# An SSM convolution by FFT with its gradients and a bilinear GLU: FFT stages in another order, buffers used in place, PSUM copies shared by ScalarE and VectorE

## Chip, cores and metric

The kernel runs on one core of one Trainium2 chip. The metric is device time in microseconds (us) of one execution of the whole program; the time of a version is the median over its runs. Engines are named as the profile names them: PE (TensorE; PEld is its weight load), DVE (VectorE), ACT (ScalarE), POOL (GpSimd), SP (SyncE, whose queue issues every DMA here).

## What is computed

One layer's forward pass and all its gradients, in bfloat16, for 2048 positions and 512 channels (F = 1376). x is normalized, passes through a long convolution (by FFT of length 4096) with a short shift filter and gates around it, and, beside that, through a bilinear GLU:

```python
def A(q, k, v, shift_k, ssm_k, ssm_D):
    k_shift = sum(k_pad[:, t:t + S, :] * shift_k[:, ks - 1 - t] for t in range(4))
    kv = k_shift * v
    y = irfft(rfft(kv, 2 * S) * rfft(ssm_k, 2 * S))[:S]
    return q * (y + kv * ssm_D)

def B(x, w_gate, w_up, w_down):
    return ((x @ w_gate) * (x @ w_up)) @ w_down

xn = layernorm(x)
out = x + A(xn, k, v, shift_k, ssm_k, ssm_D) + B(xn, w_gate, w_up, w_down)
# outputs: out, and by vjp with grad_out the gradients of
# x, k, v, shift_k, ssm_k, ssm_D, w_gate, w_up, w_down
```

Output numbers in the code: out_0 is the layer's output; out_1 to out_3 the gradients of x, k, v; out_4 of the shift filter; out_5 of ssm_k; out_6 of ssm_D (512 numbers of two bytes); out_7 to out_9 of the three weights.

## The kernel before

**Tools.** Tile pools assign buffers and every semaphore; each engine then runs its instructions in one fixed order, waiting where an instruction's input or buffer is not ready. Large tiles come from three rings of SBUF buffers, and a new tile waits until an old one of its ring has been read for the last time, by DMAs too: `s32` (four buffers), `c16` (two) and `z24` (one). PSUM tiles of the first half come from one ring of four (`ps2`).

```python
340         return main.tile(shape, dt, name=name, tag="s32", bufs=4)
343         return main.tile(shape, dt, name=name, tag="c16", bufs=2)
346         return main.tile(shape, dt, name=name, tag="z24", bufs=1)
```

**Part one, FFTs (L372 to L459).** Each transform is three steps on PE, each followed by copies out of PSUM that alternate between ACT and DVE (`evac`): `c_to_T` transposes [channel, time] data (64 transposes, 4 copies), `fwd_f1` is the first FFT factor (128 matmuls, 16 copies), `fwd_f2` the second (128 matmuls, 16 copies). Three signals are transformed: h (ssm_k, result H), kv (result KV) and dy = grad_out * xn (result DY). Order: h through all three steps; x_nat's statistics on DVE (L411) and normalization on ACT (L421, sixteen instructions), stored to xn_d for later; the shift filter as 64 matmuls with diagonal weights on k_pad (L433) into ks_C; `c_to_T` of ks_C into T_kv; v_T is loaded, multiplied into T_kv (L443); f1 and f2 of kv; xn_T and go_T are loaded and multiplied (L455); f1 and f2 of dy. The tables F2M (for f2) are made meanwhile by ACT (sines) and DVE (masks L110, copies L135, L137).

**Part two, inverses (L461 to L510).** Three times: DVE multiplies two spectra in sixteen pieces (`pointwise`), PE does `inv_i1` (copies into Bp by ACT), then `inv_i2` with table G2M, copied by ACT into y_C, dkv_C or dh_C, tiles of the c16 ring. y goes to yT_d in DRAM, dkv to dkvC_d, dh to out_5, and its first column to out_6. G2M has the z24 buffer, after F2M. Weights are loaded and transposed on PE in between: WdT (copies L504) and WT (copies L525, L528), all copied by ACT. y_nat, the transposed y, is loaded by one transposing DMA (L530) after that.

**Part three, the loop (L734 to L839).** Eight passes of 256 rows. natbuf holds rows of x, xn, grad_out (L555); PE transposes them, DVE copies them into zbuf (L565), PE multiplies by the gate and up weights (L749), ACT copies (L752), DVE forms the gated product (L758), and so on to out_0 and out_1. zbuf takes the z24 buffer. It also holds the slots A, B and C into which `apost_load` brings dkv, ks and (by a transposing DMA, L706) v; DVE works on these (L604, L613, L617, L619) to make the gradients of v, k and the shift filter. **Part four** (L843 to L895) makes the weight gradients on PE.

## Time and profile before

| | us |
|---|---|
| median of 6 runs | 756.66 (754.06 to 760.17) |
| the profiled execution | 757.93 |
| its span | 756.0 |
| PE busy | 603.1 (80%) |
| DVE busy | 427.3 (57%) |
| ACT busy | 358.3 (47%) |
| POOL busy | 16.8 (2%) |

The mean granted clock of PE over the span is 0.919 of full speed. Times in the views count from the start of the span. A busy share is a mean over parts with different limits, so the rows further down are read part by part: where the engine that ends a part sat idle, and what ended that idle time.

### The profile page before, as it was taken

The page shows a single profiled execution, that of the slowest core. Times are in us where ns is not written, and L with a number is a line of the kernel's source. Part 1 is how long each engine was busy: PE and PEld are TensorE (multiplying, and loading weights), DVE is VectorE, ACT ScalarE, POOL GpSimd, SP SyncE. Part 2 cuts the span into 40 slices and gives each one's busy share as a digit, 9 for nine tenths or more (in the row PEclk, how much of TensorE's full clock was granted, in tenths as well). Part 3 has the DMA queues.
Part 4 walks back from the last instruction along what each step waited for, and adds up shares of the span by engine and source line. Part 5 has one row for each costly group of instructions (what it writes and reads, how often), then busy time and mean ns, then how long its engine had stood idle before and what let it go on. Part 6 is the DMA issues. An engine that isn't in the chain of part 4 may idle for free.

```text
span 756.0 us, 13973 instructions
## 1 busy us (share of the span) xinstructions
PE 603.1 (80%) x5956; PEld 426.0 (56%) x5956; DVE 427.3 (57%) x952; ACT 358.3 (47%) x474; POOL 16.8 (2%) x21
## 2 busy tenths in 40 slices
...
GB/s 268 67 2 41 264 98 152 3 1 2 3 114 127 140 186 68 211 38 115 140 179 100 111 138 184 82 115 133 184 82 121 105 191 292 344 341 166 75 1 75
DMA packets 129469, 95.60 MB, mean 126 GB/s; under 512 B 78784, under 2 KB 118400, under 8 KB 129152
## 3 DMA queue, kind: packets, MB, share of 16 engines
...
## 4 chain that ended last, share of the span: by engine, by line
PE 43%; DVE 23%; DMA 12%; ACT 11%; SPq 8%; issue 2%; DVEq 0%; ACTq 0%
PE ps_wg L889 10%; PE ps_g L749 5%; PE ps_wd L878 5%; SPq L706 4%; PE ps_x L809 4%; PE ps_x L807 4%; ACT zbuf L630 3%; PE ps_o L793 3%; PE ps_n L692 3%; PE ps L207 2%; DVE pw_m L244 2%; DMA zbuf<-in_A_k_dram 2%; DVE pw_m L241 2%; DVE pw_m L242 2%; DMA zbuf<-dkvC_d 2%
## 5 line engine op out<-in xcount | busy, mean ns | idle before, releaser
L749 PE MATMUL ps_g<-zbuf,WgWu 128*128 128x256 bf16 (+1 forms) x704 | 82.0, 276 | 7.7 <-ACT btmp L752 6.7
L749 PEld LDWEIGHTS <-WgWu 128*128 128x128 bf16 (+1 forms) x704 | 70.2, 101 | 17.9 <-issue 9.2
L809 PE MATMUL ps_x<-WT,btmp 128*128 128x512 bf16 (+1 forms) x176 | 68.8, 391 | 0.0
L807 PE MATMUL ps_x<-WT,btmp 128*128 128x512 bf16 (+1 forms) x176 | 68.8, 391 | 0.0
L183 ACT CAST Bp<-ps 128x1024 bf16<-128x1024 f32 x48 | 49.9, 1103 | 35.6 <-PE ps L265 35.3
L752 ACT CAST btmp<-ps_g 128x512 bf16<-128x512 f32 x80 | 45.0, 584 | 41.3 <-PE ps_g L749 40.8
L889 PEld LDWEIGHTS <-xn_nat 128*128 128x128 bf16 x384 | 37.5, 98 | 36.9
L697 ACT COPY sf_stg<-ps_n 128x1376 bf16<-128x1376 bf16 x24 | 31.3, 1306 | 56.0 <-PE ps_n L692 50.9
L692 PE MATMUL ps_n<-ident,btmp 128*128 128x128 bf16 (+1 forms) x528 | 41.3, 222 | 16.1 <-DVE sf_stg L695 13.1
L692 PEld LDWEIGHTS <-btmp 128*128 128x128 bf16 (+1 forms) x528 | 34.0, 99 | 31.5 <-issue 13.9
L793 PE MATMUL ps_o<-WdP,btmp 128*128 128x512 bf16 (+1 forms) x176 | 44.5, 387 | 0.0
L766 PE MATMUL ps_dh<-zbuf,WdP 128*128 128x256 bf16 (+1 forms) x352 | 42.4, 272 | 0.0
L891 ACT CAST wstage<-ps_wg 128x512 bf16<-128x512 f32 (+1 forms) x24 | 13.0, 541 | 61.2 <-PE ps_wg L889 61.2
L814 ACT ACTIVATE dxn<-ps_x 128x512 f32<-128x512 f32 x16 | 9.6, 597 | 57.3 <-PE ps_x L811 37.5
L766 PEld LDWEIGHTS <-WdP 128*128 128x128 bf16 (+1 forms) x352 | 33.9, 100 | 3.4
L619 DVE SCALAR_TENSOR_TENSOR zbuf<-zbuf,wc 128x512 bf16<-128x512 bf16 x48 | 34.8, 744 | 0.4
L629 DVE TENSOR_TENSOR zbuf<-zbuf 128x512 bf16<-128x512 bf16 x64 | 23.6, 420 | 18.3 <-ACT zbuf L630 14.0
L262 PE MATMUL ps<-I1M,Y1c 128*64 128x128 bf16 x128 | 21.8, 250 | 14.9 <-DVE Y1c L245 14.9
L564 PE MATMUL ps_t<-ident,natbuf 128*128 128x128 bf16 x128 | 12.9, 230 | 23.7 <-DMA natbuf<-xn_d 21.5
L630 ACT ACTIVATE zbuf<-zbuf 128x2048 bf16<-128x2048 bf16 x16 | 30.8, 1925 | 1.6 <-DVE zbuf L629 1.6
L207 PE MATMUL ps<-BD,T_kv 128*64 128x256 bf16 x128 | 11.0, 342 | 23.5 <-DVE T_kv L443 23.5
L809 PEld LDWEIGHTS <-btmp 128*128 128x128 bf16 (+1 forms) x176 | 17.7, 100 | 19.8 <-issue 1.8
(194 smaller groups left out, 1522.6 us busy)
## 6 DMA issues: line engine op xcount, KB each, us to landing
...
h_sf<-h_n SPq DMA_DIRECT2D x2, 2048.0 KB, 9.9
dg_sf<-dg_n SPq DMA_DIRECT2D x2, 2048.0 KB, 17.1
du_sf<-du_n SPq DMA_DIRECT2D x2, 2048.0 KB, 16.6
...
```

The lines of the kernel that those rows point to most:

```text
L183: nc.scalar.copy(out=out, in_=in_)
L619: nc.vector.scalar_tensor_tensor(out=A_[:, s0:s0 + APC], in0=C_[:, s0 + j:s0 + j + APC], scalar=wc[:, t, j:j + 1], in1=A_[:, s0:s0 + APC], ...
L630: nc.scalar.activation(out=A_[:, 0:S], in_=A_[:, 0:S], func=ACTF.Copy, accum_out=dw[:, t, j:j + 1])
L692: nc.tensor.transpose(out=ps[:, ft * P:ft * P + fs], in_=XT[0:fs, ft, sl * P:(sl + 1) * P], identity=ident[0:fs, 0:fs])
L749: nc.tensor.matmul(ps[0:fs, ft - fa, :], lhsT=W[:, dt, ft * P:ft * P + fs], rhs=xg[:, 0, dt, :], start=(dt == 0), stop=(dt == NT - 1))
L752: nc.scalar.copy(out=dst[:, fa:fb, :], in_=ps[:])
L766: nc.tensor.matmul(ps[0:fs, ft - fa, :], lhsT=WdT[:, dt, ft * P:ft * P + fs], rhs=xg[:, 1, dt, :], start=(dt == 0), stop=(dt == NT - 1))
L793: nc.tensor.matmul(ps[:], lhsT=hT[0:fs, ft, sl * P:(sl + 1) * P], rhs=Wd[0:fs, ft, :], start=(ft == 0), stop=(ft == NFT - 1))
L807: nc.tensor.matmul(ps2[:], lhsT=dgT[0:fs, ft, sl * P:(sl + 1) * P], rhs=WgT[0:fs, ft, :], start=(ft == 0), stop=False)
L809: nc.tensor.matmul(ps2[:], lhsT=duT[0:fs, ft, sl * P:(sl + 1) * P], rhs=WuT[0:fs, ft, :], start=False, stop=False)
L878: nc.tensor.matmul(ps[0:fs, :], lhsT=sf_view(h_sf, h_rem, ft * P, fs)[:, st, :], rhs=go_nat[:, st, :], start=(st == 0), stop=(st == NST - 1))
L889: nc.tensor.matmul(ps[:, 0:fw], lhsT=xn_nat[:, st, dt * P:(dt + 1) * P], rhs=sf_view(main_t, rem_t, f0, fw)[:, st, :], start=(st == 0), st ...
```

## The change

Parts three and four keep their code; the rest changes so:

- The shift filter's matmuls come before f2 of h, and read and write one tile k_C (s32) in place; the upper half of each channel block is done first, and columns before time zero are skipped by shorter matmuls instead of a zeroed pad.
- v_T moves from the c16 ring to the s32 ring and is loaded right after k.
- f2 of h comes after `c_to_T` of k_C and the T_kv product's code.
- The z24 tile of part two, zinv, holds G2M and beside it io_t, into which all three inverses are copied and from which their stores read.
- y_nat is allocated and loaded right after y is stored.
- Two of the four WdT copies and half of the large WT copies go to DVE.
- A flag pool_assist lets POOL do one of the pointwise products; no line sets it.

```diff
+        self.pool_assist = False
...
-            nc.vector.tensor_tensor(out=m[3][:], in0=v(X, 1), in1=v(H, 0), op=ALU.mult)
+            (nc.gpsimd if self.pool_assist else nc.vector).tensor_tensor(out=m[3][:], in0=v(X, 1), in1=v(H, 0), op=ALU.mult)
...
-    k_pad = s32([P, NT, SP_], BF, "k_pad")
+    k_C = s32([P, NT, S], BF, "k_C")
...
+    v_T = s32([P, 64, P], BF, "v_T")
+    for t, src in enumerate(t_view(vv)):
+        nc.sync.dma_start(out=v_T[32 * t:32 * t + 32, :, :], in_=src)
...
     f.fwd_f1(T_h, A, "np")
-    H = s32([P, 128, 2, 32, 2], BF, "H")
-    f.fwd_f2(A, H)
...
-        for sc2 in range(S // 1024):
+        for sc2 in reversed(range(S // 1024)):
...
-                    nc.tensor.matmul(ps[:, u, :], lhsT=wdiag[:, t, j, :], rhs=k_pad[:, t, PAD - j + s0: PAD - j + s0 + 512],
+                    lo = j if s0 == 0 else 0
+                    nc.tensor.matmul(ps[:, u, lo:512], lhsT=wdiag[:, t, j, :], rhs=k_C[:, t, s0 + lo - j:s0 + 512 - j],
...
-            f.evac(out=ks_C[:, t, sc2 * 1024:(sc2 + 1) * 1024], in_=ps[:].rearrange("p u s -> p (u s)"))
+            f.evac(out=k_C[:, t, sc2 * 1024:(sc2 + 1) * 1024], in_=ps[:].rearrange("p u s -> p (u s)"))
...
-    v_T = c16([P, 64, P], BF, "v_T")
...
     nc.vector.tensor_tensor(out=T_kv[:], in0=T_kv[:], in1=v_T[:], op=ALU.mult)
+    H = s32([P, 128, 2, 32, 2], BF, "H")
+    f.fwd_f2(A, H)
...
-    C["G2M"] = z24([P, 64, 2, 32], BF, "G2M")
+    zinv = z24([P, 64 * 2 * 32 + NT * S], BF, "zinv")
+    C["G2M"] = zinv[:, 0:64 * 2 * 32].rearrange("p (a b c) -> p a b c", a=64, b=2)
+    io_t = zinv[:, 64 * 2 * 32:].rearrange("p (t s) -> p t s", t=NT)
...
+    f.inv_i2(Bp, io_t)
+    nc.sync.dma_start(out=yT_d.rearrange("(t p) s -> p t s", p=P), in_=io_t)
+    y_nat = c16([P, NST, D], BF, "y_nat")
+    nc.sync.dma_start_transpose(out=y_nat[:], in_=yT_d[:, :])
...
-        nc.scalar.copy(out=WdT[:, dt, :], in_=ps[:, 0:FF])
+        (nc.scalar.copy if dt % 2 == 0 else nc.vector.tensor_copy)(out=WdT[:, dt, :], in_=ps[:, 0:FF])
...
-                nc.scalar.copy(out=WT[:, w, f4:f4 + nfull, :], in_=ps[:, 0:nfull, :, :].rearrange("p a b c -> p a (b c)"))
+                (nc.scalar.copy if (f4 // 4 + w) % 2 == 0 else nc.vector.tensor_copy)(
+                    out=WT[:, w, f4:f4 + nfull, :], in_=ps[:, 0:nfull, :, :].rearrange("p a b c -> p a (b c)"))
```

The diff does not show where the scheduler puts each instruction. Three places of DVE's order do. The first is the start, around the two T_h copies (PSUM to SBUF after `c_to_T` of h); ln_stats and ln_mv belong to x_nat's statistics, cb_mi are index masks. Before:

```order
L110 TENSOR_SCALAR cb_mi_158<-cb_mi_158 128x32
L185 COPY T_h<-ps_258 128x2048
L411 BN_STATS ln_stats<-x_nat 128x6 x2
L110 TENSOR_SCALAR cb_mi_171<-cb_mi_171 128x1024
L185 COPY T_h<-ps_294 128x2048
```

Now:

```order
L412 BN_STATS ln_stats<-x_nat 128x6
L110 TENSOR_SCALAR cb_mi_176<-cb_mi_176 128x1024
L413 BN_AGGR ln_mv<-ln_stats 128x2 x2
L412 BN_STATS ln_stats<-x_nat 128x6 x2
L135 COPY F2M<-cb_resb_179 64x16x64 x2
L413 BN_AGGR ln_mv<-ln_stats 128x2 x2
L412 BN_STATS ln_stats<-x_nat 128x6
L110 TENSOR_SCALAR cb_mi_187<-cb_mi_187 128x1024
L186 COPY T_h<-ps_263 128x2048
L186 COPY T_h<-ps_299 128x2048
```

One T_h copy stood ahead of all statistics and the other behind one pair of them; now seven BN_STATS (three of them ahead of the rows shown) and two masks precede both.

The second place is the middle: from the last copies of T_kv to the first transform of kv. Before:

```order
L185 COPY T_kv<-ps_830 128x2048
L81 TENSOR_SCALAR cb_mi_1547<-cb_mi_1547 128x1024
L443 TENSOR_TENSOR T_kv<-T_kv,v_T 128x8192
L185 CAST A_kv<-ps_865 128x64x16
L185 CAST A_kv<-ps_885 128x64x16
```

Now:

```order
L186 COPY T_kv<-ps_672 128x2048
L186 CAST H<-ps_702 128x2x128x4
L186 CAST H<-ps_722 128x2x128x4
L81 TENSOR_SCALAR cb_mi_1545<-cb_mi_1545 128x1024
L186 CAST H<-ps_742 128x2x128x4
L440 TENSOR_TENSOR T_kv<-T_kv,v_T 128x8192
L186 CAST H<-ps_762 128x2x128x4
L186 CAST H<-ps_782 128x2x128x4
```

DVE's eight copies of H now lie around the T_kv product, three ahead of it and five behind; on PE, f2 of H lies between `c_to_T` of k_C and f1 of kv.

The third place is the start of the loop; the names behind "waits" are semaphores (DMAHW0 to 7 count DMAs, others an engine's instructions). Before:

```order
L611 MEMSET zbuf 128x8 [waits PE_49]
L604 TENSOR_TENSOR zbuf<-zbuf 128x512 [waits DMAHW7_49,DMAHW0_49]
L604 TENSOR_TENSOR zbuf<-zbuf 128x512 x3
L613 TENSOR_TENSOR zbuf<-zbuf 128x512 [waits DMAHW1_49]
L613 TENSOR_TENSOR zbuf<-zbuf 128x512 x3
L617 TENSOR_SCALAR zbuf<-zbuf,wc 128x512 [waits DVE_49] x2
L796 TENSOR_TENSOR a_t<-natbuf,y_nat 128x512 [waits DMAHW4_49,DMAHW3_49]
L619 SCALAR_TENSOR_TENSOR zbuf<-zbuf,wc 128x512 [waits DVE_49]
L803 TENSOR_TENSOR dxa<-natbuf,y_nat 128x512 [waits DMAHW4_49]
L565 COPY zbuf<-ps_t 128x8x128 [waits PE_49,Activation_49]
```

Now:

```order
L526 COPY WT<-ps_4273 128x1024 [waits PE_49]
L565 COPY zbuf<-ps_t 128x8x128 [waits DMAHW3_49,DMAHW4_49,DMAHW0_49,DMAHW6_49,PE_49,Activation_49]
L611 MEMSET zbuf 128x8
L565 COPY zbuf<-ps_t 128x8x128 [waits DVE_49,PE_49]
L604 TENSOR_TENSOR zbuf<-zbuf 128x512 [waits DMAHW6_49,DMAHW5_49]
L604 TENSOR_TENSOR zbuf<-zbuf 128x512 x3
L613 TENSOR_TENSOR zbuf<-zbuf 128x512 [waits DMAHW7_49]
L613 TENSOR_TENSOR zbuf<-zbuf 128x512 x3
L617 TENSOR_SCALAR zbuf<-zbuf,wc 128x512 [waits DVE_49] x2
L619 SCALAR_TENSOR_TENSOR zbuf<-zbuf,wc 128x512 [waits DVE_49] x6
L617 TENSOR_SCALAR zbuf<-zbuf,wc 128x512 x2
L758 TENSOR_TENSOR btmp<-btmp 128x2560 [waits Activation_49]
```

The two L565 copies moved ahead of the work on the slots; the first of them is now the first write into zbuf and waits for DMAs (DMAHW3 and DMAHW4 count those of out_6 and out_5), and L758 follows six of the twelve L619. On SP's queue the six natbuf loads moved from behind L706 to right behind y_nat's load.

## Rows read from the trace of the kernel before

**Rows 1.** The chain that ended last, in order of time: start us, us, engine, output.

```profile
72.41 7.53 DMA xn_d<-x_nat
...
88.80 10.67 DMA v_T<-in_A_v_dram
...
123.84 9.77 DMA go_T<-in_grad_out_dram
...
290.39 19.89 SPq L706
...
319.63 11.12 PE ps_g L749 x84
```

**Rows 2.** Timeline of PE, 54 to 116: start, us, instruction, [idle before <-releaser].

```profile
54.70 14.00 PE L433 MATMUL ps<-k_pad,wdiag 128*128 128x512 bf16 x64
...
74.24 6.45 PE L194 MATMUL ps<-ident,ks_C 128*128 128x128 bf16 x64 [5.53 <-ACT ks_C L183]
...
104.16 10.99 PE L207 MATMUL ps<-BD,T_kv 128*64 128x256 bf16 x128 [23.47 <-DVE T_kv L443]
```

**Rows 3.** Timeline of ACT: x_nat normalized, and the WdT copies.

```profile
61.00 11.38 ACT L421 ACTIVATE x_nat<-x_nat,ln_nmr,rstd 128x512 bf16<-128x512 bf16 x16
...
276.07 4.93 ACT L504 COPY WdP<-ps 128x1376 bf16<-128x1376 bf16 x4 [5.12 <-PE ps L503]
```

**Rows 4.** Timeline of SP's queue: start, us of issue, line, transfer, count.

```profile
106.84 13.62 SPq L451 DMA_DIRECT2D xn_T<-xn_d  x4
...
285.61 0.40 SPq L510 DMA_DIRECT2D out_dram<-dh_C  x1
...
288.36 0.39 SPq L508 DMA_DIRECT2D out_dram<-dh_C  x1
```

**Rows 5.** DMA issues: transfer, queue, kind, count, KB, median us to landing.

```profile
ksC_d<-ks_C SPq DMA_DIRECT2D x1, 2048.0 KB, 12.0
...
yT_d<-y_C SPq DMA_DIRECT2D x1, 2048.0 KB, 8.5
...
out_dram<-dh_C SPq DMA_DIRECT2D x1, 2048.0 KB, 18.1
...
zbuf<-in_A_v_dram SPq DMA_TRANSPOSE x4, 6.7
...
y_nat<-yT_d SPq DMA_TRANSPOSE x1, 14.1
...
out_dram<-dh_C SPq DMA_DIRECT2D x1, 1.0 KB, 16.0
```

**Rows 6.** Timeline of DVE: statistics, mask, F2M copies, go_T product, zbuf copy, gating product.

```profile
17.63 1.28 DVE L411 BATCH_NORM_STATS2 ln_stats<-x_nat 128x6 f32<-128x512 bf16 x2
...
19.52 0.69 DVE L110 TENSOR_SCALAR cb_mi<-cb_mi 128x1024 int32<-128x1024 int32 x1 [0.61 <-ACT cb_mi L109]
...
22.59 0.85 DVE L135 COPY F2M<-cb_resb 64x1024 bf16<-64x1024 bf16 x2
...
133.93 4.43 DVE L455 TENSOR_TENSOR go_T<-go_T,xn_T 128x8192 bf16<-128x8192 bf16 x1 [2.05 <-DMA go_T<-in_grad_out_dram]
...
316.97 0.69 DVE L565 COPY zbuf<-ps_t 128x1024 bf16<-128x1024 bf16 x1 [0.32 <-PE ps_t L564]
...
331.40 1.49 DVE L758 TENSOR_TENSOR btmp<-btmp 128x2560 bf16<-128x2560 bf16 x1 [5.07 <-ACT btmp L752]
```

**Rows 7.** Busy time by stretch: stretch, us, engines busy, PEclk, DMA share, GB/s.

```profile
21.40:35.00 13.60, 11.31 (x128) 9.83 (x128) 13.40 (x21) 13.02 (x13) 1.05 (x1) 1.00 0.30 55
116.40:131.90 15.50, 14.15 (x128) 12.44 (x128) 9.80 (x9) 8.10 (x8) 0.00 (x0) 1.00 1.38 155
215.00:238.00 23.00, 18.52 (x411) 15.37 (x405) 23.00 (x69) 14.92 (x16) 0.00 (x0) 0.85 0.24 93
300.00:306.50 6.50, 0.00 (x0) 0.00 (x0) 0.00 (x0) 0.00 (x0) 0.00 (x0) 0.50 0.93 322
```

**Rows 8.** Costliest groups of instructions, from the page: the L619 chain.

```profile
L619 DVE SCALAR_TENSOR_TENSOR zbuf<-zbuf,wc 128x512 bf16<-128x512 bf16 x48 | 34.8, 744 | 0.4
```

More of the change, by code (lines that the diff above doesn't have):

```diff
@@ L439 @@
     f.c_to_T(ks_v, T_kv)
-    v_T = c16([P, 64, P], BF, "v_T")
-    for t, src in enumerate(t_view(vv)):
-        nc.sync.dma_start(out=v_T[32 * t:32 * t + 32, :, :], in_=src)
     nc.vector.tensor_tensor(out=T_kv[:], in0=T_kv[:], in1=v_T[:], op=ALU.mult)
-    A = s32([P, 2, 32, 256], BF, "A_kv")
-    f.fwd_f1(T_kv, A, "np")
+    H = s32([P, 128, 2, 32, 2], BF, "H")
+    f.fwd_f2(A, H)
+    A2 = s32([P, 2, 32, 256], BF, "A_kv")
+    f.fwd_f1(T_kv, A2, "np")
     KV = s32([P, 128, 2, 32, 2], BF, "KV")
-    f.fwd_f2(A, KV)
+    f.fwd_f2(A2, KV)
     xn_T = s32([P, 64, P], BF, "xn_T")
@@ L473 @@
         f.inv_i1(Y1, Bp, jq0=j0 // 8, jq1=(j0 + JC) // 8, jbase=j0)
-    y_C = c16([P, NT, S], BF, "y_C")
-    f.inv_i2(Bp, y_C[:])
-    nc.sync.dma_start(out=yT_d.rearrange("(t p) s -> p t s", p=P), in_=y_C[:])
+    f.inv_i2(Bp, io_t)
+    nc.sync.dma_start(out=yT_d.rearrange("(t p) s -> p t s", p=P), in_=io_t)
+    y_nat = c16([P, NST, D], BF, "y_nat")
+    nc.sync.dma_start_transpose(out=y_nat[:], in_=yT_d[:, :])
     Bp = s32([P, 64, 2, 128], BF, "Bp2")
@@ L480 @@
         f.inv_i1(H, Bp, jq0=j0 // 8, jq1=(j0 + JC) // 8)
-    dkv_C = c16([P, NT, S], BF, "dkv_C")
-    f.inv_i2(Bp, dkv_C[:])
-    nc.sync.dma_start(out=dkvC_d, in_=dkv_C[:])
+    f.inv_i2(Bp, io_t)
+    nc.sync.dma_start(out=dkvC_d, in_=io_t)
     WgWu = s32([P, 2, NT, FF], BF, "WgWu")
```

14 lines of the change are left out of this document (4 added, 10 removed).

## The prediction

> **What bounds the kernel now.** I read the chain of waits in order of time first, because it names the stretches where nothing computes; then each engine's timeline around those stretches; then the DMA issues, for what the waits wait on. The tail (weight gradients) and most of the eight-pass loop are PE work that the diff does not touch. The diff touches what comes before the loop's first matmul at 319.63 [rows 1]. There the chain shows three holes.
>
> Hole one: the transposes of the shifted k (L194) begin at 74.24, having sat idle 5.53 us for the last ks_C copies [rows 2]. These stood on ACT behind the sixteen x_nat normalizations, 11.38 us from 61.00 [rows 3]. Hole two: the next matmuls start at 104.16 after 23.47 us of idle [rows 2]. Their input waits for v_T, whose DMA takes over x_nat's buffer and so follows the store of xn_d: 7.53 us of store, and a last piece of v_T that takes 10.67 us, both on the chain [rows 1]. Hole three: before 319.63 the natbuf loads stand on SP's queue behind the transposing load L706, whose issue alone took 19.89 us [rows 1]. L706 stands behind the stores of out_6 and out_5, which landed 16.0 and 18.1 us after their issues at 285.61 and 288.36 [rows 4, 5].
>
> **The first part: c_to_T of ks earlier.** The convolution moves ahead of the second FFT step of H. All times now are places on the old time axis. The new DVE order puts seven BN_STATS, two index masks and two F2M copies ahead of both T_h copies; the old one put one T_h copy first. Seven at 0.64 (1.28 for two), two masks at 0.69, the F2M pair 0.85 and 0.7 for the small rest are 7.4 us [rows 6]; two T_h copies at the usual 1.2 follow. They start when x_nat is there: after 14.9, where DVE's old small work ended, and by 17.63, where the old order read it. So f1 of h, which needs all of T_h, starts between 24.7 and 27.4; I take 26.0 against 21.40, a cost of 4.6. It keeps its length of 13.6, since the same copies pace it [rows 7]: to 39.6. The convolution follows at once. Its 64 matmuls took 14.00 [rows 2], 1.75 for each of eight tiles. ACT copies tiles 0, 2 and 4 and then normalizes x_nat: tile 4 is ready at 48.4, copied by about 49.6 (an ACT copy is 8.10 / 8 = 1.0 [rows 7]), x_nat is done 11.4 later at 61.0, the last k copy at 62.1. So c_to_T starts at 62.1 instead of 74.24: **12.1 gained**. This is not the whole 16 us of the moved step, because the statistics now delay T_h and x_nat still stands in front of the last copy. In-place evacuation of k_C adds no wait: a tile only overwrites columns that PE has read, the upper half first.
>
> **The second part: from there to the dy transform.** Old: 74.24 to the end of the go_T product, 133.93 + 4.43 = 138.4, which is 64.2. New, in PE's order: c_to_T 6.45 [rows 2]; f2 of H at full clock 14.15 for 16 tiles, as KV took [rows 7]; f1 of kv 10.99 [rows 2]; the old gap of 1.3 before f2; f2 of KV 14.15; the last copy 1.2; the product 4.43 [rows 6]. That is 52.7. The product T_kv*v_T (4.43) runs beside f2 of H, but in the middle of DVE's H copies, and only four PSUM tiles exist: DVE owes eight copies of 1.2 (9.80 in KV's stretch [rows 7]) and the product, 14.0, in a stretch of 14.15, with the product in one block. I count 2.5 us of PE stalled there (zero at best, 4.4 at worst). 55.2 in all, **9.0 gained**; dy starts at 117.3 instead of 138.4.
>
> What could be late instead: v_T is issued right behind k and has landed long before 75. The go_T and xn_T loads need xn_d stored (61.1 + 7.53 = 68.6) and, for xn_T, the buffer of k_C, free when ksC_d is stored (62.1 + 12.0 = 74.1) [rows 1, 5]. Four xn_T issues took 13.62 and the old set of eight needed from 104.04 to 133.6, some 29.6, ending with a 9.77 landing [rows 1, 4]. From 74.1 that ends at 104, and the product wants it at 112.8: hidden, with 9 us to spare.
>
> **The third part: into the loop.** The inverse transforms and pointwise products are unchanged; the moves in them are hidden. y_nat (14.1 to land [rows 5]) is transposed right after y is stored, where DVE is busy 23.00 of 23.00 us with pointwise products and the DMA engines 0.24 [rows 7]; without that cover it would cost those 14. On SP it stands ahead of the natbuf and weight loads, of which nothing is needed before the third inverse. zinv makes the second and third inverse's copies wait for the store of the one before; yT_d landed in 8.5 [rows 5], under the same 23 us of DVE work, or it would cost 8.5 each. Two of the four WdT copies, 4.93 together, go to DVE [rows 3]: the i2 copies start 1.0 earlier. The WT copies split too, behind which nothing now waits.
>
> The new wait is the one that matters. zbuf takes the only z24 buffer, which the old kernel had free when PE had read G2M. Now zinv also holds what out_6 and out_5 read, so the first write into zbuf (L565, and the load L704) waits for both to land. On the old axis: 288.36 - 1.0 + 18.1 = 305.5. The natbuf loads are in long before, and L565 now stands ahead of L604 on DVE. From L565 (316.97) to L749 (319.63) was 2.66 [rows 1, 6], so L749 starts at 308.2: 11.4 earlier. The loads L704 to L706 now go out at 305.5; the transposing one took 6.7 as a median [rows 5], so L613 can start near 313.7, and it, L617 and six of the L619 (0.74 each, 0.70 apart [rows 8]) hold DVE to 320.6. The gating product L758 stands behind them; PE would have it ready at 308.2 + 11.8 = 320.0. So 320.6 against 331.40 [rows 6]: 10.8. Six L619 are left for the first pass, 4.2 us in a DVE that is not full; I charge 1.5 (0 to 4.2). **9.3 gained.**
>
> Here the trace and a rule bear on each other. A 2 MB store of the same kind, yT_d, landed in 8.5; out_5, issued behind out_6, took 18.1 [rows 5]. Between 300.0 and 306.5 the DMA engines moved 322 GB/s [rows 7], so out_5's bytes went late. The Trainium skill, "DMA: Bandwidth & Descriptors", section "Queues, rings and completion order", says that a transfer's semaphore increment lands only after every earlier write from that DMA engine; its "Specifications" add that pieces under 512 B are read, modified and written. By that rule, which speaks against the new wait, out_6's two-byte pieces hold out_5 in the changed kernel too, and the third part stays at 9.3; with out_5 alone as fast as yT_d it would be 18.4. The trace agrees with the rule so far.
>
> **Sum.** 12.1 + 9.0 + 9.3 = 30.4. The profiled execution took 757.93 (span 756.0 and 1.93 around it), so 727.5; the median of the runs shown is 1.27 below it: **726.3 us**.
>
> **Rivals.** (a) *The convolution runs at half clock.* For: PE now idles some 6 us before f1 of h, and the clock row shows 0.50 after long idling [rows 7]. Against: f1 itself ran at 1.00 with PE busy 11.31 of 13.6, and the convolution follows without a gap. Price: a tile takes 3.5 instead of 1.75, tile 4 is 8.7 later, the first part is 3.4: 735.0. (b) *out_5 lands as quickly as yT_d.* L565 goes at 295.9, the third part becomes 18.4: 717.2. The rows above speak against it. (c) *The transposing load stays slow.* If L706's issue takes 19.89 again, DVE's L613 waits until 327 and more, L758 with it to some 336, and the third part turns into a loss of 6: 741.6. Against: those 19.89 stood behind out_5 on the same queue, which has now landed before L706 is issued. (d) *Slower: the zbuf wait.* Every microsecond that out_5 lands later than 18.1 after its issue moves the loop by one. The loop's own gain is gone at some 29, all gain at 48.5; at 55 the time is 763. Nothing in the trace shows a store that slow, but two-byte pieces did slow this one, and no other wait that the change adds lies on the path. (e) That the change does not do what it says is partly certain: pool_assist is never set, so POOL multiplies nothing; that is in the sum as zero.
>
> **How the numbers follow.** Forecast 0.65, (a) 0.14, (b) 0.10, (c) 0.07, (d) 0.04. The range of 715 to 739 holds the forecast, (a), (b) and the bounds of the unknowns: first part 3.4 to 16.7 (T_h not delayed), second 7 to 11.5, third 6.6 to 18.4. About 0.5%, 4 us, is what a measurement of this kernel tells from no change. Faster by more: 0.95; within: 0.02; slower: 0.03, all from (d).
>
> **What would show it.** Right: PE's transposes of k_C near 62; no idle before f1 of kv; f1 of dy near 117; the first L565 some 21 us before 305.5, released by a store's DMA. Wrong: x_nat starting after 53 (first part), more than 5 us of PE idle within f2 of H (second), the first L749 released by anything but L565 or later than 290 (third), or a loop that is longer than before by more than 3 us.

## The result, and the profile after

| | before | after |
|---|---|---|
| median of the runs | 757.54 (16 runs) | 723.68 (8 runs) |
| ratio to before, with its 95% interval | | 0.956 (0.954 to 0.958) |
| the profiled execution | 757.93 | 727.22 |
| its span | 756.0 | 725.4 |
| mean granted clock of PE | 0.919 | 0.939 |
| PE, DVE, ACT busy | 603.1, 427.3, 358.3 | 599.2, 431.1, 351.6 |

The changed kernel is 33.9 us faster by the medians and 30.7 by the two profiled executions; the forecast was 30.4 less, 726.3. The profiled execution of the changed kernel is 3.5 us above its median, so what is read from the traces below adds up to the smaller of the two gains. The engines are about as busy as before (the last row), so the gain is idle time that went. In one of the experiments (run 8, statistics held back) the profiled execution ran at a mean granted clock of 0.649; of PE's times only the start of the first step of h is read from it, and over its first 20 us the clock was 0.93.

The first two holes are read on PE's timeline (start, length, operation; in brackets the idle time just before it and what ended it). These rows answer to [rows 2]; the last one is the first step of dy, at 138.4 before:

```profile
26.72 6.16 PE L208 MATMUL ps<-BD,T_h 128*64 128x256 bf16 x56 [7.03 <-ACT T_h L184]
...
40.56 14.00 PE L433 MATMUL ps<-k_C,wdiag 128*128 128x512 bf16 x64
62.66 6.50 PE L195 MATMUL ps<-ident,k_C 128*128 128x128 bf16 x64 [8.09 <-ACT k_C L184]
...
84.05 10.23 PE L208 MATMUL ps<-BD,T_kv 128*64 128x256 bf16 x128
...
115.40 11.48 PE L208 MATMUL ps<-BD,go_T 128*64 128x256 bf16 x128 [5.65 <-DVE go_T L455]
```

The transposes of k (L195) start at 62.66 instead of 74.24, still after 8.09 us of idling for the last k copy. The 23.47 us in front of the first step of kv are gone: it starts at 84.05 with no wait. dy starts at 115.40. What stands in front of the last k copy is ACT's block of sixteen normalizations, as in [rows 3]:

```profile
50.33 11.38 ACT L422 ACTIVATE x_nat<-x_nat,ln_nmr,rstd 128x512 bf16<-128x512 bf16 x16
61.61 0.99 ACT L184 CAST k_C<-ps 128x1024 bf16<-128x1024 f32 x1
```

DVE's timeline shows the two products, neither of which waits now, and the loop's first write into zbuf, which waits 14.96 us for a store from zinv. These rows answer to [rows 6]:

```profile
75.74 4.41 DVE L440 TENSOR_TENSOR T_kv<-T_kv,v_T 128x8192 bf16<-128x8192 bf16 x1
...
110.93 4.41 DVE L455 TENSOR_TENSOR go_T<-go_T,xn_T 128x8192 bf16<-128x8192 bf16 x1
...
283.21 0.69 DVE L565 COPY zbuf<-ps_t 128x1024 bf16<-128x1024 bf16 x1 [14.96 <-DMA out_dram<-zinv]
...
292.46 1.43 DVE L613 TENSOR_TENSOR zbuf<-zbuf 128x512 bf16<-128x512 bf16 x4 [1.96 <-DMA zbuf<-in_A_v_dram]
...
298.84 1.48 DVE L758 TENSOR_TENSOR btmp<-btmp 128x2560 bf16<-128x2560 bf16 x1
```

SP's queue issues the store of out_6, then that of out_5, and then nothing until both are done; the transposing load L706, 19.89 us before [rows 1], takes 4.88:

```profile
262.13 0.40 SPq L511 DMA_DIRECT2D out_dram<-zinv  x1
264.88 0.38 SPq L509 DMA_DIRECT2D out_dram<-zinv  x1
283.13 0.34 SPq L704 DMA_DIRECT2D zbuf<-dkvC_d  x1
...
284.00 4.88 SPq L706 DMA_TRANSPOSE zbuf<-in_A_v_dram  x1
```

In the chain of waits (start, length, what) the out_5 store is now a link of its own, and near the end the load of go_nat is another, which was not on the chain before; there the row was a store of dg_n of 11.07 us:

```profile
264.88 18.11 DMA out_dram<-zinv
...
284.00 8.44 DMA zbuf<-in_A_v_dram
...
298.92 1.40 DVE btmp L758
...
591.28 12.78 DMA go_nat<-in_grad_out_dram
604.20 40.46 PE ps_wd L878 x176
644.67 74.36 PE ps_wg L889 x384
```

To compare places in the loop with those of before, I take the issue of WdP's load as a mark, since the code between it and the loop is nearly the same: 268.00 before, 245.46 after, so 22.5 us earlier. The gating product L758 is 32.6 us earlier (331.40 to 298.84), which leaves 10.0 to the third part. From the third pass on it is 31.1 to 32.0 earlier (31.7 in the last), and the last stage 30.5 (675.21 to 644.67). There one wait took the place of another: before, the last pass stood 11.07 us for the store of dg_n, and PE's next matmuls ran at half clock (granted 0.50 from 628 to 633); now PE idles 6.2 us for go_nat and begins ps_wd at a granted clock of 0.50, which is the 1.2 GHz level. The windows (stretch, length, busy time of PE, its weight load, DVE, ACT and POOL, then granted clock, DMA share, GB/s) show it:

```profile
598.00:604.20 6.20, 0.00 (x1) 0.03 (x1) 1.70 (x5) 1.50 (x3) 0.00 (x0) 0.83 1.07 376
604.20:607.00 2.80, 2.80 (x7) 0.99 (x8) 0.43 (x1) 0.00 (x0) 0.00 (x0) 0.50 1.08 379
607.00:612.00 5.00, 5.00 (x20) 2.08 (x19) 0.00 (x0) 0.58 (x1) 0.00 (x0) 0.81 1.10 359
```

### The profile page after: what moved, and what is told of

Read it like the earlier page. It is cut to its first block, busy times and chain, and to the rows that moved or that the text cites. A ratio compares the mean times of both kernels' runs of the same rounds, so it can differ in the third digit from the quotient of the medians.

```text
span 725.4 us, 13991 instructions
## 1 busy us (share of the span) xinstructions
PE 599.2 (83%) x5956; PEld 422.2 (58%) x5956; DVE 431.1 (59%) x956; ACT 351.6 (48%) x469; POOL 16.8 (2%) x21
## 4 chain that ended last, share of the span: by engine, by line
PE 41%; DVE 21%; DMA 11%; ACT 7%; SPq 2%; issue 2%; DVEq 0%; ACTq 0%
PE ps_wg L889 10%; PE ps_wd L878 6%; PE ps_g L749 4%; PE ps_x L809 4%; PE ps_x L807 4%; ACT zbuf L630 3%; PE ps_o L793 3%; PE ps_n L692 3%; DMA out_dram<-zinv 2%; DVE pw_m L245 2%; DMA zbuf<-in_A_k_dram 2%; DVE pw_m L242 2%; DVE pw_m L243 2%; DMA zbuf<-dkvC_d 2%; SPq L706 2%; DMA go_nat<-in_grad_out_dram 2%
## 5 line engine op out<-in xcount | busy, mean ns | idle before, releaser
L749 PE MATMUL ps_g<-zbuf,WgWu 128*128 128x256 bf16 (+1 forms) x704 | 82.9, 278 | 7.3 <-ACT btmp L752 6.5
L749 PEld LDWEIGHTS <-WgWu 128*128 128x128 bf16 (+1 forms) x704 | 70.7, 102 | 17.9 <-issue 8.6
L809 PE MATMUL ps_x<-WT,btmp 128*128 128x512 bf16 (+1 forms) x176 | 68.2, 387 | 0.0
L807 PE MATMUL ps_x<-WT,btmp 128*128 128x512 bf16 (+1 forms) x176 | 67.5, 383 | 0.0
L766 PEld LDWEIGHTS <-WdP 128*128 128x128 bf16 (+1 forms) x352 | 33.9, 100 | 3.4
L878 PE MATMUL ps_wd<-go_nat,h_sf 128*128 128x512 bf16 x128 | 30.1, 401 | 6.2 <-DMA go_nat<-in_grad_out_dram 6.2
L619 DVE SCALAR_TENSOR_TENSOR zbuf<-zbuf,wc 128x512 bf16<-128x512 bf16 x48 | 34.7, 744 | 0.4
L770 ACT CAST dh_sb<-ps_dh 128x512 bf16<-128x512 f32 x40 | 22.7, 595 | 12.4 <-PE ps_dh L766 8.1
## 6 DMA issues: line engine op xcount, KB each, us to landing
h_sf<-h_n SPq DMA_DIRECT2D x2, 2048.0 KB, 10.7
du_sf<-du_n SPq DMA_DIRECT2D x2, 2048.0 KB, 16.6
```

Source lines behind the costliest of these rows:

```text
L619: nc.vector.scalar_tensor_tensor(out=A_[:, s0:s0 + APC], in0=C_[:, s0 + j:s0 + j + APC], scalar=wc[:, t, j:j + 1], in1=A_[:, s0:s0 + APC], ...
L749: nc.tensor.matmul(ps[0:fs, ft - fa, :], lhsT=W[:, dt, ft * P:ft * P + fs], rhs=xg[:, 0, dt, :], start=(dt == 0), stop=(dt == NT - 1))
L766: nc.tensor.matmul(ps[0:fs, ft - fa, :], lhsT=WdT[:, dt, ft * P:ft * P + fs], rhs=xg[:, 1, dt, :], start=(dt == 0), stop=(dt == NT - 1))
L807: nc.tensor.matmul(ps2[:], lhsT=dgT[0:fs, ft, sl * P:(sl + 1) * P], rhs=WgT[0:fs, ft, :], start=(ft == 0), stop=False)
L809: nc.tensor.matmul(ps2[:], lhsT=duT[0:fs, ft, sl * P:(sl + 1) * P], rhs=WuT[0:fs, ft, :], start=False, stop=False)
L878: nc.tensor.matmul(ps[0:fs, :], lhsT=sf_view(h_sf, h_rem, ft * P, fs)[:, st, :], rhs=go_nat[:, st, :], start=(st == 0), stop=(st == NST - 1))
```

## The experiments

The theory is the prediction's: three parts, 12.1 from the earlier transposes of k, 9.0 from there to dy, 9.3 into the loop, with the last one held down by the wait for out_6 and out_5. Against it: that the early load of v_T, not the new order, carries the front (runs 1 and 2); that the late part is worth nothing without the early one (3); that out_5 is slow by itself (4 and 5). Later runs test what sets the two waits that were left, and a version that takes them out. Medians are given with the ratio to the kernel before on the same chip; after stands at 0.956. The kernel before had medians of 754.65 to 757.54 in these sets, so a difference between the medians of two runs holds to some 3 us, and the ratios are the safer comparison.

### 1. The order undone

```diff
     f.fwd_f1(T_h, A, "np")
+    H = s32([P, 128, 2, 32, 2], BF, "H")
+    f.fwd_f2(A, H)
...
     nc.vector.tensor_tensor(out=T_kv[:], in0=T_kv[:], in1=v_T[:], op=ALU.mult)
-    H = s32([P, 128, 2, 32, 2], BF, "H")
-    f.fwd_f2(A, H)
```

> The changed kernel with one edit: the second FFT step of H stands ahead of the convolution again, as in the kernel before. v_T stays early in its own buffer, everything else as changed. Theory A (the prediction's first part: the moved step brings the convolution and the transposes of k forward by some 12 us): the transposes of k start at 62.7 + 14.2, less the 8.1 us that PE now idles there, so at some 69 to 74; the product and the first step of kv then follow with nothing beside them but the product, so what was gained comes back as a loss of 5 to 10: 729 to 734 us. Theory B (the move itself is worth little; v_T's early load is what removed the 23.5 us hole): the H step fills the 8.1 us in which PE waits for the last k copy, the first step of kv starts within 3 us of 84.05, and the time is 721 to 727 us. Transposes of k near 70 and kv near 83 decide for B; kv later than 89 for A.

Measured: 726.75 us, ratio 0.9603 (0.9586 to 0.962); 3.1 more than the changed kernel. PE's timeline has the transposes of k 12 us later than in the changed kernel, as theory A says, but the first step of kv only 2.4:

```profile
74.71 5.94 PE L195 MATMUL ps<-ident,k_C 128*128 128x128 bf16 x64 [2.25 <-DVE k_C L186]
86.48 11.09 PE L208 MATMUL ps<-BD,T_kv 128*64 128x256 bf16 x128 [5.83 <-DVE T_kv L442]
```

B holds. The H step now fills the time in which PE otherwise idles for the last k copy (8.09 us), and PE idles behind the transposes instead, 5.83 us for the product. So the new order by itself is worth some 3 us, as long as v_T is there.

### 2. v_T late

```diff
-    v_T = s32([P, 64, P], BF, "v_T")
...
     f.c_to_T(ks_v, T_kv)
+    v_T = c16([P, 64, P], BF, "v_T")
+    for t, src in enumerate(t_view(vv)):
+        nc.sync.dma_start(out=v_T[32 * t:32 * t + 32, :, :], in_=src)
```

> The changed kernel with one edit: v_T is loaded where the kernel before loaded it, into x_nat's 16 KB buffer, behind the store of xn_d. Order of the steps as changed. Theory B (the early load carries the front's gain): the load cannot start before xn_d is stored (61.7 + 7.5 = 69.3), needs 20 us as before (88.9), the product 4.4, so the first step of kv starts at 93 to 95 instead of 84.05; go_T then gets T_kv's buffer, free only when that step is done, and its product comes 10 to 15 us later than 110.9: 733 to 741 us. Theory A (the order carries it): kv within 5 us of 84.05 and under 730 us.

Measured: 734.15, ratio 0.970 (0.9678 to 0.9721); 10.5 more than the changed kernel. The product with v_T waits 6.80 us for the load, and kv starts at 92.17; on PE's timeline

```profile
21.47 6.95 PE L208 MATMUL ps<-BD,T_h 128*64 128x256 bf16 x72 [1.78 <-ACT T_h L184]
...
52.73 5.95 PE L195 MATMUL ps<-ident,k_C 128*128 128x128 bf16 x64 [2.01 <-DVE k_C L186]
...
92.17 11.26 PE L208 MATMUL ps<-BD,T_kv 128*64 128x256 bf16 x128 [12.87 <-DVE T_kv L440]
```

and on DVE's:

```profile
87.69 4.42 DVE L440 TENSOR_TENSOR T_kv<-T_kv,v_T 128x8192 bf16<-128x8192 bf16 x1 [6.80 <-DMA v_T<-in_A_v_dram]
```

kv is 1 us better than B's range, the time inside it. Two things came along that I had not asked for: the scheduler put the T_h copies first again, so the first step of h starts at 21.47, and all k copies ahead of x_nat, so the transposes of k start at 52.73, ten microseconds earlier than in the changed kernel. None of that reaches the end, since v_T is late. x_nat's block, behind which v_T's load waits, starts 2.5 us later (52.79 instead of 50.33), so the order alone is not measured quite cleanly here.

### 3. The late part alone

The kernel before, with the diff's lines for zinv, io_t, y_nat and the WdT and WT copies, and nothing of the front.

> The kernel before with the late edits alone: inverse results in zinv, y_nat transposed early, natbuf in its own buffer, WdT and WT copies split; the front is untouched. Theory (the prediction's third part): 9.3 us gained, with the first L749 some 11 after-change microseconds nearer to the third inverse; the trace of the changed kernel puts it at 9.6 to 10 and the tail gives about 2 back, so 746.5 to 750 us (ratio to before 0.986 to 0.990). Rival (the late part needs the early one, or was worth nothing by itself): 755 to 759. Rival (the late part carries more than half of the whole gain): under 742.

Measured: 746.10, ratio 0.9867 (0.9828 to 0.9905): 10.7 us gained by the medians, 0.4 past the theory's range and far from both rivals. The first write into zbuf waits 15.05 us for a store there too, and L758 is at 319.36 instead of 331.40:

```profile
319.36 1.49 DVE L758 TENSOR_TENSOR btmp<-btmp 128x2560 bf16<-128x2560 bf16 x1
```

1.2 of these 12.0 were there at the mark, the issue of WdP's load (266.80, from 268.00). What each of the late edits (zinv, the early y_nat, the natbuf loads ahead of L706, the shared copies) gives alone was not run. With the runs before, the front can be taken apart, from 746.1: the order without the early v_T gives 12.0 (run 2), the early v_T without the order 19.4 (run 1), both 22.4, each to some 3 us. They cover the same hole, so their gains don't add.

### 4. out_6 later, a miss

```diff
-        nc.sync.dma_start(out=out_6.rearrange("(t p) -> p t", p=P), in_=io_t[:, :, 0])
+    dh0 = cpool.tile([P, NT], BF, name="dh0")
+    nc.vector.tensor_copy(out=dh0[:], in_=io_t[:, :, 0])
...
         nc.sync.dma_start(out=out_4.rearrange("(t p) j -> p t j", p=P), in_=dw_b[:])
+        nc.sync.dma_start(out=out_6.rearrange("(t p) -> p t", p=P), in_=dh0[:])
```

> The changed kernel with one edit: the first column of dh is copied to a small tile, and out_6 is stored from there after the eight passes, not ahead of out_5. Theory C (the 512 two-byte pieces of out_6 hold out_5 back): out_5 lands 8 to 9 us after its issue instead of 18.1, the first write into zbuf follows at some 273.5 instead of 283.2, the loads and the whole loop come 9 to 10 us earlier: 713 to 716 us. Rival D (out_5 is slow by itself, as a store to an output or behind something else): it lands 17 to 19 us after its issue and the time is 722 to 725 us. Between: the gain stops at what is next, PE's transposes into natbuf's PSUM tile, ready at 270.9, or the transposing load (8.4 us).

Measured: 724.42, ratio 0.9576 (0.9539 to 0.9613). The edit did not do what it was for: the store's input was ready early, so the scheduler issued it at 261.91, still ahead of out_5 at 264.45, which took 17.8 us. It decides nothing.

### 5. out_6 in four pieces

```diff
-        nc.sync.dma_start(out=out_6.rearrange("(t p) -> p t", p=P), in_=io_t[:, :, 0])
+    ps6 = f.ps2([P, P], BF)
+    nc.tensor.transpose(out=ps6[0:NT, :], in_=io_t[:, :, 0], identity=ident[:])
+    dh0 = cpool.tile([P, P], BF, name="dh0")
+    nc.vector.tensor_copy(out=dh0[0:NT, :], in_=ps6[0:NT, :])
+    nc.sync.dma_start(out=out_6.rearrange("(t p) -> t p", p=P), in_=dh0[0:NT, :])
```

> The changed kernel with one edit: the first column of dh is transposed on PE and out_6 stored from four partitions, in 4 pieces of 256 bytes instead of 512 pieces of 2. (The run before this one tried to store out_6 later, but its issue stayed ahead of out_5's, so it told nothing.) Theory C (the small pieces hold out_5 back): out_5 lands 8 to 9 us after its issue instead of 18.1, the first write into zbuf comes 9 to 10 us earlier, and so does the loop: 713 to 716 us. Rival D (out_5 is slow by itself): 17 to 19 us again, 722 to 725 us.

Measured: 711.93, ratio 0.9424 (0.9387 to 0.9462): 11.8 us less than the changed kernel by the medians, some 10 by the ratios, and at least what C had asked for. The four pieces are still issued ahead of out_5 (260.94 and 263.17), so the order is the same and only the pieces differ. Its chain of waits, beside the 18.11 us of the changed kernel:

```profile
263.17 6.58 DMA out_dram<-zinv
...
285.67 1.40 DVE btmp L761
...
593.36 38.15 PE ps_wd L881 x176
```

out_5 lands 6.58 us after its issue; the gating product (L761 in this file) is at 285.67 instead of 298.92. C holds: the 512 pieces of two bytes held 2 MB for 11.5 us. The rest of the 13.2 is that out_5 was issued 1.7 earlier in this execution. The windows (the last number is GB/s) show how, first two of the changed kernel, then one of this run:

```profile
268.00:278.00 10.00, 0.61 (x8) 0.49 (x8) 0.25 (x1) 2.25 (x2) 0.00 (x0) 0.65 0.78 17
278.00:282.00 4.00, 0.00 (x0) 0.00 (x0) 0.00 (x0) 0.00 (x0) 0.00 (x0) 0.50 0.84 337
```

```profile
264.00:270.00 6.00, 3.06 (x45) 2.77 (x43) 2.13 (x4) 4.54 (x5) 0.00 (x0) 0.86 0.87 350
```

With the small pieces almost nothing moved for ten microseconds, although the DMA engines were busy (0.78); out_6 landed at 277.6, and some 1.3 of out_5's 2 MB moved only then.

### 6. out_4 behind the last loads

```diff
+    with nc.allow_non_contiguous_dma(reason="tiny output"):
+        tc.keep_in_program_order(nc.sync.dma_start(out=out_4.rearrange("(t p) j -> p t j", p=P), in_=dw_b[:]))
```

(placed behind the three load_sf calls, and taken away in front of go_nat)

> The changed kernel with one edit: out_4, the other store in small pieces (512 of 8 bytes), is issued behind the loads of the last stage instead of just ahead of go_nat. Theory C (small pieces hold the next transfers): go_nat, which took 12.78 us and ends last before the first ps_wd matmul, lands in 7 to 9, and ps_wd starts 4 to 6 us earlier: 718 to 720 us. Rival (go_nat is slow because the 2 MB load of h_sf runs beside it): it takes 12 to 13 again and the time is 722 to 725.

Measured: 729.66, ratio 0.966 (0.962 to 0.970), slower by 6.0 than the changed kernel. The edit moved more than it should: the second load of h_sf now went out at 584.32, ahead of go_nat, whose issue came at 594.77 and which took 10.79 with no out_4 in front. So go_nat is long without out_4's pieces too, and C's 7 to 9 did not come; but neither did the rival's 12 to 13. That other loads beside it make it long is not shown, and how much out_4's pieces add can't be read from this run.

### 7. x_nat on DVE

```diff
-        nc.scalar.activation(out=x_nat[:, st, :], in_=x_nat[:, st, :], func=ACTF.Identity,
-                             scale=rstd[:, st:st + 1], bias=nmr[:, st:st + 1])
+        nc.vector.tensor_scalar(out=x_nat[:, st, :], in0=x_nat[:, st, :], scalar1=rstd[:, st:st + 1],
+                                scalar2=nmr[:, st:st + 1], op0=ALU.mult, op1=ALU.add)
```

> The changed kernel with one edit: the sixteen normalizations of x_nat run on DVE, not on ACT. Theory (the 8.09 us hole ahead of the transposes of k is the x_nat block of 11.38 us standing in front of the last ACT copy): a DVE multiply of this size took 0.27 to 0.33, sixteen 4.3 to 5.3, so the last k copies are done at 55 to 56.5 and the transposes start there instead of at 62.66; everything to the dy transform moves along by 6 to 7, go_T's loads too: 716 to 718.5 us. Rival (something else is late right behind, as go_T or the H copies): the transposes are early but dy less than 3 us earlier than 115.4, 721 to 724 us.

Measured: 722.94, ratio 0.9566 (0.9531 to 0.960): no gain. The block took 6.56 us on DVE (expected 4.3 to 5.3), the transposes of k came 4.7 us earlier, at 58.00, and yet the first step of kv only 1.7, as PE's timeline shows:

```profile
58.00 6.44 PE L195 MATMUL ps<-ident,k_C 128*128 128x128 bf16 x64 [3.93 <-DVE k_C L186]
...
82.32 10.69 PE L208 MATMUL ps<-BD,T_kv 128*64 128x256 bf16 x128 [3.90 <-DVE T_kv L440]
```

DVE's timeline has the reason:

```profile
49.03 6.56 DVE L422 TENSOR_SCALAR x_nat<-x_nat,rstd,ln_nmr 128x512 bf16<-128x512 bf16 x16
...
77.85 4.42 DVE L440 TENSOR_TENSOR T_kv<-T_kv,v_T 128x8192 bf16<-128x8192 bf16 x1
```

The rival holds. The product with v_T stands in DVE's fixed order behind seven H copies; it starts at 77.85, 2 us later than in the changed kernel, and PE waits 3.90 for it; dy starts at 114.12, 1.3 earlier. The hole was moved, not removed.

### 8. Statistics held back, x_nat on DVE

```diff
-        nc.vector.bn_stats(out=stats[:, st, :], in_=x_nat[:, st, :])
+        bs = nc.vector.bn_stats(out=stats[:, st, :], in_=x_nat[:, st, :])
+        tc.keep_in_program_order(bs)
```

with the edit of run 7.

> The changed kernel with two edits: the statistics of x_nat are held behind the copies of the first step of h on DVE, so that T_h is not delayed, and the normalizations run on DVE. Theory (the statistics ahead of the T_h copies cost what the prediction charged, some 5 us, and x_nat another 7): the first step of h starts at 21 to 22 instead of 26.72, the transposes of k at 50 to 52 instead of 62.66; then DVE owes eight H copies, the product and 4.3 to 5.3 of x_nat in the H step, 18 to 19 us instead of 14.15, so the first step of kv starts at 75 to 78 instead of 84.05: 714 to 718 us. Rival (the statistics now fill the time in which DVE should copy k): the transposes come later than 56 and it is no better than the run with the second edit alone.

Measured: ratio 0.9609 (0.9559 to 0.9659), not told apart from the changed kernel or from run 7, and above the theory's 714 to 718 us. All statistics now stood behind the T_h copies on DVE, and the first step of h still began at 26.25, as in run 7, where they stood ahead. DVE's row of the two T_h copies is the same in both runs:

```profile
23.18 2.33 DVE L186 COPY T_h<-ps 128x2048 bf16<-128x2048 bf16 x2
```

So taking the statistics away gained nothing: where they had stood, DVE now waits for what ACT builds for the tables, 2.76 us for the first mask, 1.21 for F2M's copies and 0.42 for the second mask, all ahead of its T_h copies. On ACT the first T_h copy began at 21.53, behind builders of F2M too (21.52 in run 7). In the changed kernel's trace all this is 0.5 later; there x_nat landed 0.7 later, and with it the statistics ahead of the first mask.

### 9. T_h first on both engines

```diff
-    cb.build_f2m(C["F2M"], 0)
...
     f.c_to_T(h_C[:], T_h)
+    with tc.issue_after(f.last_act.ins):
+        cb.build_f2m(C["F2M"], 0)
...
+    with tc.issue_after(th_dve):
+        for st in range(NST):
```

(the second build_f2m and build_i1m move along; last_act and th_dve are the last T_h copies on ACT and DVE; the loop is that of the statistics)

> The changed kernel with two ordering edits: on ACT the builders of F2M and I1M are held behind the T_h copies, on DVE the statistics are. Nothing else moves by hand. Theory E (T_h was late because ACT's first T_h copy stood behind three builder instructions, 16.4 to 22.0, and not, as the prediction said, because of the statistics on DVE, which the run before this had already taken away without effect): the first step of h starts at 21 to 22 instead of 26.72 and the convolution at 35 instead of 40.56. The transposes of k then start at 51 to 56, since all four ACT copies now stand ahead of x_nat; but x_nat's 11.4 us fall ahead of the T_kv copies, so the first step of kv gains only 1 to 4 us on 84.05: 719.5 to 723 us. Rival (T_h's start is set by something else, as the identity or the load of h): 26 again, and 722 to 725.

Measured: 720.80, ratio 0.9553 (0.9516 to 0.959). The medians are 2.9 apart, which these intervals don't settle; dy starts at 112.15 instead of 115.40. ACT's timeline of the changed kernel, and then of this run, shows what stood in front of T_h:

```profile
16.39 1.27 ACT L109 ACTIVATE cb_mi<-cb_bi,cb_c,cb_pc_f 128x1024 int32<-128x1024 int32 x1
19.67 1.15 ACT L97 ACTIVATE cb_resb<-cb_mi,cb_c 128x1024 bf16<-128x1024 int32 x1 [2.01 <-DVE cb_mi L110]
20.85 1.24 ACT L109 ACTIVATE cb_mi<-cb_bi,cb_c,cb_pc_f 128x1024 int32<-128x1024 int32 x1
22.00 1.84 ACT L184 COPY T_h<-ps 128x2048 bf16<-128x2048 bf16 x1
```

```profile
16.33 3.87 ACT L184 COPY T_h<-ps 128x2048 bf16<-128x2048 bf16 x2
...
53.69 11.43 ACT L425 ACTIVATE x_nat<-x_nat,ln_nmr,rstd 128x512 bf16<-128x512 bf16 x16 [2.38 <-DVE ln_nmr L423]
65.03 3.60 ACT L184 COPY T_kv<-ps 128x2048 bf16<-128x2048 bf16 x2
```

PE's timeline of this run:

```profile
21.16 3.17 PE L208 MATMUL ps<-BD,T_h 128*64 128x256 bf16 x40 [1.36 <-ACT T_h L184]
...
53.72 5.91 PE L195 MATMUL ps<-ident,k_C 128*128 128x128 bf16 x64 [1.77 <-DVE ln_nmr L423]
...
80.80 10.24 PE L208 MATMUL ps<-BD,T_kv 128*64 128x256 bf16 x128
```

E holds as far as the builders go: on ACT three instructions of the table builder, with a wait of 2.01 us for a mask, stood ahead of the first T_h copy; with the builders behind the T_h copies the first step of h starts at 21.16. But DVE's two T_h copies were as late in the changed kernel, behind the builders' masks and F2M copies:

```profile
23.66 2.33 DVE L186 COPY T_h<-ps 128x2048 bf16<-128x2048 bf16 x2
```

They ended at 25.99, ACT's at 26.66. This edit moves the builders' DVE instructions too (the first of these masks runs at 23.51, behind both copies), so whether ACT's order alone would do is not shown. The transposes of k follow at 53.72, but x_nat's 11.43 us now stand in front of the T_kv copies, and kv starts 3.2 us earlier only.

### 10. A first version meant to beat both

out_6 as in run 5, T_h first as in run 9, x_nat on DVE as in run 7, and:

```diff
-    nc.vector.tensor_tensor(out=T_kv[:], in0=T_kv[:], in1=v_T[:], op=ALU.mult)
+    for a in range(4):
+        pr = nc.vector.tensor_tensor(out=T_kv[:, 16 * a:16 * a + 16, :], in0=T_kv[:, 16 * a:16 * a + 16, :],
+                                     in1=v_T[:, 16 * a:16 * a + 16, :], op=ALU.mult)
...
-    f.fwd_f2(A, H)
+    with tc.issue_after(pr.ins):
+        f.fwd_f2(A, H)
```

> A version meant to beat both: the changed kernel with out_6 in four pieces, the T_h copies first as in the run before, x_nat's normalizations on DVE, and the product with v_T in four parts with DVE's H copies held behind it. Theory: 11.8 us from out_6 as measured, and the first step of kv at 76 to 79 instead of 84.05, all of which reaches the dy transform if go_T's loads are not late: 704 to 708 us. Rival 1 (the product ahead of the H copies stalls PE as long as it saved): 709 to 713. Rival 2 (go_T or xn_T late: its product waits for a DMA): dy less than 4 us earlier than 115.4, 708 to 712.

Measured: 711.74, ratio 0.9431 (0.9406 to 0.9455), no better than run 5 alone. kv started at 84.01: in DVE's order two index masks came to stand in front of the product, the second waited 4.94 us for ACT, and the product began at 69.00 although T_kv had been copied at 62.9, with the H copies behind it. Rival 1, with that wait as its cause.

### 11. The switch set

```diff
     f.evac_engines = ("act",)
+    f.pool_assist = True
```

> The changed kernel with the switch set that the change adds and never sets: in the three pointwise stages the fourth product of each chunk runs on POOL. DVE is busy without a gap there at 2.01 us a chunk, 48 chunks. Theory: POOL's price for 128 x 512 lies between 0.3 us (the index fill of 1024 took 0.60) and 0.9 (twice the memset's 0.86 ns an element), hidden beside DVE's other products, so each chunk is 0.34 to 0.41 shorter: 16 to 20 us less, 704 to 708. Rival (POOL's multiply is longer than the rest of a chunk, over 1.6 us, or slows DVE's operations beside it): the chunk is POOL's length, 724 to 760 us or more.

Measured: 753.15, ratio 0.9963 (0.9936 to 0.9991): 29.5 slower than the changed kernel, nearly all of its gain. The groups of instructions (count, then busy time and mean ns of one), first POOL's, then DVE's product beside it:

```profile
L245 POOL TENSOR_TENSOR pw_m<-KV,H 128x512 bf16<-128x512 bf16 x16 | 20.4, 1278 | 103.5 <-DVE zinv L162 84.6 <-DVE Y1c L250 18.8
...
L243 DVE TENSOR_TENSOR pw_m<-KV,H 128x512 bf16<-128x512 bf16 x16 | 22.0, 1372 | 0.0
...
L242 DVE TENSOR_TENSOR pw_m<-KV,H 128x512 bf16<-128x512 bf16 x16 | 6.6, 414 | 0.1
```

POOL's multiply takes 1.28 us (1.20 and 1.21 in the two later stages), which would fit beside the chunk's 2.01. (The 0.60 us of the expectation was a mean over index fills of several sizes; the fill of 128x1024 took 1.06.) But the DVE product that runs beside it takes 1.37 instead of 0.41, and after the first chunk only that one: by these two lengths DVE stood still while POOL worked. 1.37 - 0.41 less the 0.34 that moved away is 0.62 a chunk, and 48 chunks are 29.8.

The Trainium skill, "SBUF — State Buffer", section "SBUF: two separate sides", says that POOL and a DVE operation with two SBUF inputs take one shared pair of ports for a whole instruction each, the other one blocked. The trace agrees, with 1.37 beside 1.28.

### 12. A second version

Runs 5 and 9 together, the product whole again, and x_nat shared:

```diff
+        if st % 2 == 0:
+            nc.scalar.activation(out=x_nat[:, st, :], in_=x_nat[:, st, :], func=ACTF.Identity,
+                                 scale=rstd[:, st:st + 1], bias=nmr[:, st:st + 1])
+        else:
+            nc.vector.tensor_scalar(out=x_nat[:, st, :], in0=x_nat[:, st, :], scalar1=rstd[:, st:st + 1],
+                                    scalar2=nmr[:, st:st + 1], op0=ALU.mult, op1=ALU.add)
```

> A second version meant to beat both: the changed kernel with out_6 in four pieces (11.8 us by itself), the T_h copies first on ACT and DVE (2.9 by itself), and x_nat's sixteen normalizations shared, eight on ACT and eight on DVE; the product stays whole, where the scheduler puts it. Theory: the two measured gains add, 709; x_nat is done at 60 instead of 65, ACT's T_kv copies with it, so the first step of kv starts at 76 to 79 instead of 80.8 and go_T's loads are as much earlier: 705 to 709 us. Rival (the DVE half of x_nat delays DVE's T_kv copies and the product, as in the run before): kv at 81 to 84, 709 to 713 us.

Measured: 707.08, ratio 0.9337 (0.930 to 0.9375): 16.6 us less than the changed kernel, the fastest of all. PE's timeline:

```profile
53.59 6.46 PE L195 MATMUL ps<-ident,k_C 128*128 128x128 bf16 x64 [1.77 <-DVE ln_nmr L423]
...
77.38 10.23 PE L208 MATMUL ps<-BD,T_kv 128*64 128x256 bf16 x128 [1.92 <-DVE T_kv L447]
...
108.72 11.23 PE L208 MATMUL ps<-BD,go_T 128*64 128x256 bf16 x128 [5.65 <-DVE go_T L462]
```

kv starts at 77.38 and dy at 108.72, 6.7 earlier than in the changed kernel; the theory holds.

## Why the prediction was right, point by point

The time came within 3 us of the forecast, and so did each part. But one term was right for a wrong reason, and the split between order and load was not seen. From the traces, 11.6 and 11.4 for the first two parts, less 0.5 on the way to the mark, 10.0 for the third and 2.0 lost behind the loop's first pass are the 30.5 of the last stage.

**The first part** forecast 12.1 (transposes at 62.1 instead of 74.24); it gave 11.6, at 62.66. The step "seven BN_STATS, two index masks and two F2M copies ahead of both T_h copies" failed in its cause, though not in its size: DVE's T_h copies ended at 25.99 and the first step of h began at 26.72, where I had 26.0. But the statistics, 4.5 of the 7.4 us that I charged, cost next to nothing (runs 7 and 8): without them DVE waits as long for what ACT builds for the masks and F2M. And ACT's T_h copies, which I had not looked at, stood behind three builder instructions and ended last, at 26.66. What held T_h was the table builders on both engines; with them behind the copies the step starts at 21.16 (run 9). I had compared the two orders on DVE only, and took the first difference that had the right size. That the size came out was luck. What follows in that part held: convolution 14.00 at full clock, x_nat from 50.33 (49.6), last k copy at 61.61 and done by 62.6 (62.1).

**The second part** forecast 9.0; it gave 11.4 (52.7 instead of 64.2 from the transposes to dy). Of the 2.5 us charged for a stall of PE in the H step only 0.9 were there: the step ran from 68.99 to 84.05, 0.9 more than 14.15, though the product stood as one block among the H copies. This term was too large. f1 of kv took 10.23, not 10.99. go_T was in time, as forecast.

What both parts missed is what they have in common. The sum gave the order 12.1 and the rest 9.0, and a reader would think the order worth more. Runs 1 to 3 show that v_T's early load without the order gives 19.4 of the 22.4, the order without the load 12.0, and the order on top of the load 3. Run 2, which is behind the 12.0, had another order of the copies on ACT and DVE as well, so that share is the least certain. The sum was right only because both edits are made.

**The third part** forecast 9.3; by run 3 alone it is 10.7 (7 to 13 by its interval), by the trace 10.0 at L758, of which 1.0 is given back by the next reading two passes later (31.5 there), against 1.5 charged. On the old axis, with the mark's 22.5, the first zbuf write is at 305.7 (305.5 forecast), L749 at 308.3 (308.2), L613 at 315.0 (313.7) and L758 at 321.4 (320.6). The WdT copies gave 0.9 (from WdP's issue to out_6's, 17.61 to 16.67); they were not run by themselves.

**The rule on the store.** I left the third part at 9.3 because out_6's pieces would hold out_5. Run 5 shows that they do: 18.11 us with them, 6.58 with four. Its windows show in what way: 17 GB/s until 278, 337 after it. So most of out_5's bytes themselves went late, as I had read from [rows 7], and not only the signal that they had landed.

The Trainium skill, "DMA: Bandwidth & Descriptors", section "Queues, rings and completion order", gave the rule that an increment lands only after the earlier writes; the trace agrees that out_5 landed behind out_6 (283.0 and 277.6), but by that rule alone the bytes need not have been late, and here they were.

**Rivals.** (a) The convolution ran at full clock: 14.00 us for 64 matmuls. (b) out_5 landed no sooner than before. Its price had a slip: from 305.5 to 295.9 are 9.6, so 18.9 and 716.7 us, not 18.4 and 717.2. (c) The transposing load took 4.88 in its issue and 8.44 to land, not 19.89. (d) out_5 took 18.11, its deciding point was 48.5. (e) pool_assist cost and gave nothing, and run 11 shows that it is better unset.

**Not foreseen:** go_nat. Beyond the loop I had no term. There the wait for go_nat took the place of the wait for the dg_n store. ps_wd starts 32.9 earlier than before (637.07 to 604.20), more than the last L758 (31.7), but begins at half clock and takes 2.3 longer, so the last stage keeps 30.5.
